# Re-timing six things in a one-core GFNet and mixer kernel: three loads, one store, the filter copies, one fetch, one batch of x, and the stage-1 slots

## The chip, the cores and the metric

One core of one Trainium2 chip. The metric is device time in microseconds (us), from one execution; a kernel was run several times in rounds with the other, and a time quoted alone is the median. Engines: PE (TensorE), DVE (VectorE), ACT (ScalarE), POOL (GpSimd), SP (SyncE, which here only issues transfers). The chip also records the clock that it granted TensorE, as a share of full speed (0.984 on the mean in the kernel before).

## The reference, cut to what matters

```python
def _attn_ref(x, filt_r, filt_i):              # x: 8 x 3136 x 256
    X = np.fft.rfft(x, axis=1)
    Y = X * (filt_r + 1j * filt_i)[None, :, :]
    return np.fft.irfft(Y, n=x.shape[1], axis=1)

def _moe_ref(x, U, V, w_ch1, w_ch2):           # rank 32, hidden 1024
    h = x.transpose(0, 2, 1) @ U @ V
    u = x + h.transpose(0, 2, 1)
    return u + np.maximum(u @ w_ch1, 0.0) @ w_ch2

# reference = _moe_ref(_attn_ref(x, filt_r, filt_i), ...)
```

## The kernel before

The transform of length 3136 = 64 x 49 is split into four matmul stages. Stage 1 (L305) turns x into `asb`, stored to DRAM (`ct1`); stage 2 (L400) reads it back as `a`; VectorE, or GpSimd for some chunks, multiplies with the filter (`uv`, or `ta`, `tb` and their sum `y`); stage 3 (L392) gives `esb`, stored to `ct2`; stage 4 (L592) reads that back as `e`, with the low-rank part `h` in 32 extra rows, and gives `ut`, which feeds the channel matmuls (L603, relu on ScalarE, L636).

The program has one main loop, over blocks of 512 tokens with eight steps each. Each step has one piece of the channel matmuls of batch b; work of later batches is put into steps by a plan. So TensorE's instruction order is fixed, and a late input stops everything behind it: in the kernel before it stood idle for 3.69 us ahead of the matmul at 56.91, until x had come.

```python
    # banks: "w" is ONE bank, used by stage 4 and by stage 1 of batches 2 to 7
    of = {"m": (0, 1), "o": (2, 3), "w": (4,), "e": (7,), ..., "u": (5, 6)}[tag]

    def load_x(b, c, after=None):          # on GpSimd's queue
        ...
            if after is not None:          # a one-element copy: not before `after` is there
                nc.gpsimd.tensor_copy(t[0:1, 0, 0:1], after)
            for h in range(2):
                nc.gpsimd.dma_start(t[h:128:2, ...], dram(x.tensor, ...))

    def st1(b, by=()):                     # stage 1, a generator: one unit per step
        tag = "u" if b == 1 else "w"
        for c in range(3):
            ...                            # 2 matmuls into one bank, copied out to asb
            for h in range(2):
                (nc.gpsimd if (b, c) == (1, 2) else nc.sync).dma_start(dram(ct1[b], ...), asb[...])
            if 2 < b < NB - 1 and c:
                load_x(b + 1, c - 1)       # x of the next batch, from batch 3 on
            yield
        ...

    def make_fc(k, copy):  copy(fc[0:NR, ...], fb[64:NZ, ...])            # L406
    def make_neg(k):       nc.vector.tensor_scalar_mul(fc[64:NZ, ...], fb[64:NZ, ...], -1.0)   # L409
    def make_fa(k, copy):  copy(fa[64:NZ, ...], fb[0:NR, ...])            # L412

    def mid_first():                       # batch 0, before the main loop
        ...
                if k == 7:
                    load_e2(0, 1, 64, 48)
                    load_e2(0, 2)
                    nc.sync.dma_start(sv[0:64, 1024:], s4_d[:, 1024:])
                    load_e2(0, 6)

    def put_h(b, c):                       # the 32 rows of h: e<-h, L559
        nc.vector.tensor_copy(t[64:96], free(h1[b], 64, 96, 0, [[0, n], [1, DM]]))

    # in plan_mid(b, s): when the first three chunks a of batch b are fetched
        for k in range(3):
            at(later(s, (-7, -5, -5)[k] if b == 2 else -8 if b == 3 else -9), fetch, k)

    # the plan
    for n, k in ((9, 3), (10, 5), (11, 2), (12, 4), (13, 0), (13, 1), (15, 6), (15, 7)):
        at(n, make_neg, k)
    for n, k in ((12, 3), (12, 5), (14, 2), (14, 4)):
        at(n, make_fa, k, nc.vector.tensor_copy)
    for n, k in ((6, 0), (7, 1), (8, 6), (9, 7)):
        at(n, make_fc, k, nc.gpsimd.tensor_copy)
    for b in range(1, NB):
        if b == 2:
            plan_st1(b, 18, (0, 3, 4, 5, 7))        # slots: step of the block, 0 to 7
        elif b > 2:
            plan_st1(b, later(start[b - 1], -42 if b == 3 else -60), (0, 3, 4, 5, 7) if b == 3 else (0, 4, 7))
        m = later(start[b - 1], (16, -2, -10, -12)[min(b, 4) - 1])
        ...
    # stage 4 of the next block stands in steps 2 and 6 of a block
```

## Time and profile before

| | before |
|---|---|
| time, 3 runs | 558.71 us (557.92 to 559.39) |
| span of the profiled run | 557.3 us |
| TensorE busy / idle in it | 520.8 / 36.5 us |
| granted clock, mean | 0.984 |

The views: the page gives busy time per engine and, in 40 slices of the span, the tenths of the granted clock. A timeline line has a start, a duration, engine, source line, operation, tiles and shapes, how many instructions are merged, and in brackets the idle time ahead of them with the instruction that ended it. "The gate" stands for the halved clock of the windows view (0.50 from 55.11 to 61.94 in the kernel before). The prediction shows TensorE's lines. Two more turn out to matter. First, VectorE's timeline of the kernel before:

```profile
58.25 0.69 DVE L559 COPY e<-h 32x2048 f16<-32x2048 f16 x1
...
62.70 0.41 DVE L409 TENSOR_SCALAR fc<-fb 49x1024 f16<-49x1024 f16 x1
...
64.16 2.23 DVE L409 TENSOR_SCALAR fc<-fb 49x1024 f16<-49x1024 f16 x1
```

And GpSimd's timeline of the kernel before, over the same time:

```profile
62.61 1.47 POOL L313 DMA_DIRECT2D ct<-asb  x2 [6.06 <-issue]
64.08 2.02 POOL L406 COPY fc<-fb 49x1024 f16<-49x1024 f16 x2
```

One negation takes 0.41 us, the other 2.23 us; the slow one lies beside GpSimd's two copies. And GpSimd does nothing for 6.06 us ahead of the store at 62.61: the store waits for its data, and the two copies behind it wait with it. In just this pause VectorE copies `e<-h` in 0.69 us.

### The profile page before, as it was taken

The numbers are of one execution on the slowest core, as the hardware profiler recorded it, in microseconds if no ns is written. First come the engines' busy times: TensorE is split into PE (matmuls) and PEld (weight loads), VectorE is DVE, ScalarE is ACT, GpSimd is POOL, SyncE is SP. The second block draws the span as 40 slices with busy tenths as digits, with TensorE's granted clock in tenths as the row PEclk, the third lists the DMA queues.
The fourth block names the chain that finished last, engine by engine and source line by source line (L and its number), as shares of the span: only waits on it lengthen the run. The fifth ranks groups of instructions, "written<-read, shape, count | busy, mean of one in ns | idle before, by whom it ended". The sixth has DMA issues, their size and how long they took to land.

```text
span 557.3 us, 11729 instructions
## 1 busy us (share of the span) xinstructions
PE 520.8 (93%) x4540; PEld 374.2 (67%) x4540; DVE 353.7 (63%) x414; ACT 374.9 (67%) x677; POOL 281.3 (50%) x205
## 2 busy tenths in 40 slices
PE   5896879989998889998999999999999999999996
PEld 3643546666675657776776777777786777777775
DVE  7984756637546737669746785758746887643332
ACT  4655437756877567776876788767777567765663
POOL 6856359517995157914684175816563297300000
PEclk9999779999999989999999999999999999999999
DMA  9999496469859749954879468865754554343212
GB/s 195 166 193 211 123 213 181 132 184 194 225 156 193 207 120 221 221 154 126 210 211 234 123 172 219 166 192 159 193 165 124 141 161 126 107 113 114 96 76 85
DMA packets 84391, 91.96 MB, mean 165 GB/s; under 512 B 6725, under 2 KB 68440, under 8 KB 84336
## 3 DMA queue, kind: packets, MB, share of 16 engines
q1 hardware_dynamic: 66560, 74.49, 45.7%
q0 software_dynamic: 17072, 16.26, 19.3%
q8 instruction: 35, 0.57, 0.4%
q10 hardware_dynamic: 704, 0.46, 0.3%
q14 instruction: 20, 0.16, 0.1%
HBM read 57.12 MB, written 49.77 MB: 192 GB/s over the span
## 4 chain that ended last, share of the span: by engine, by line
PE 57%; POOL 2%; DVE 2%; ACT 1%; issue 1%; DMA 1%; ACTq 0%; POOLq 0%
PE psum L636 21%; PE psum L603 21%; PE psum L612 3%; PE psum L400 3%; PE psum L592 3%; PE psum L392 3%; PE psum L305 2%; POOL y L736 1%; PE psum L530 1%; DVE e L559 1%; DMA a<-ct 1%; DVE ut L597 1%; POOL x L187 0%; DVE tb L734 0%; DVE tb L732 0%
## 5 line engine op out<-in xcount | busy, mean ns | idle before, releaser
L607 ACT ACTIVATE hring<-psum 128x512 f16<-128x512 f32 (+1 forms) x416 | 238.1, 576 | 118.7 <-PE psum L603 117.2
L603 PE MATMUL psum<-ut,w1sb 128*128 128x512 f16 (+1 forms) x832 | 242.5, 373 | 2.4 <-DVE ut L597 1.9
L636 PE MATMUL psum<-w2sb,hring 128*128 128x256 f16 x1536 | 231.7, 274 | 0.0
L636 PEld LDWEIGHTS <-hring 128*128 128x128 f16 x1536 | 143.6, 98 | 65.0 <-issue 5.3
L736 POOL TENSOR_TENSOR y<-ta,tb 113x1024 f16<-113x1024 f16 x52 | 111.9, 2158 | 136.5 <-DVE tb L734 91.5
L597 DVE CAST ut<-psum 128x512 f16<-128x512 f32 x94 | 69.6, 741 | 103.3 <-PE psum L592 84.2
L603 PEld LDWEIGHTS <-w1sb 128*128 128x128 f16 x832 | 104.7, 145 | 24.1 <-issue 6.3
L644 DVE COPY och<-psum 128x512 f32<-128x512 f32 x96 | 66.1, 689 | 54.3 <-PE psum L612 53.6
L370 ACT CAST esb<-psum 98x512 f16<-98x512 f32 x128 | 75.0, 587 | 22.8 <-PE psum L392 17.2
L612 PE MATMUL psum<-idn,ut 128*128 128x128 f16 x392 | 54.0, 219 | 0.0
L309 ACT CAST asb<-psum 128x512 f16<-128x512 f32 x76 | 44.8, 589 | 12.3 <-PE psum L305 11.4
L730 DVE TENSOR_TENSOR ta<-psum,fb 113x1024 f16<-113x1024 f32 x37 | 45.1, 1218 | 9.0 <-PE psum L400 7.8
L592 PEld LDWEIGHTS <-e 96*128 96x128 f16 x752 | 34.5, 97 | 23.6 <-issue 6.3
L732 DVE TENSOR_TENSOR tb<-psum,fc 49x1024 f16<-49x1024 f32 x37 | 45.4, 1226 | 1.0
L734 DVE TENSOR_TENSOR tb<-psum,fc 49x1024 f16<-49x1024 f32 x37 | 45.1, 1218 | 1.0
L400 PE MATMUL psum<-a,w2t 98*128 98x512 f16 x120 | 37.1, 386 | 7.6 <-DMA a<-ct 2.9
L592 PE MATMUL psum<-sv,e 96*128 96x64 f16 x752 | 37.3, 192 | 5.0 <-DMA e<-ct 1.9
L612 PEld LDWEIGHTS <-ut 128*128 128x128 f16 x392 | 38.5, 98 | 4.9
L730 POOL TENSOR_TENSOR ta<-pc,fb 113x1024 f16<-113x1024 f16 x15 | 32.4, 2159 | 16.7 <-ACT pc L740 16.6
L305 PE MATMUL psum<-x,wf 128*128 128x256 f16 x168 | 32.7, 280 | 7.4 <-DMA x<-in_x_dram 4.5
L392 PE MATMUL psum<-y,g 113*98 113x512 f16 x98 | 37.4, 381 | 2.2 <-POOL y L736 1.2
L187 POOL DMA_DIRECT2D x<-in_x_dram x48 | 31.1, 661 | 5.1 <-DMA w1sb<-in_moe_w_ch_dram 3.1
(112 smaller groups left out, 385.8 us busy)
## 6 DMA issues: line engine op xcount, KB each, us to landing
out_dram<-och SPq DMA_DIRECT2D x47, 512.0 KB
ct<-esb SPq DMA_DIRECT2D x64, 196.0 KB
x<-in_x_dram POOLq DMA_DIRECT2D x48, 256.0 KB, 7.7
e<-ct SPq DMA_DIRECT2D x46, 256.0 KB
a<-ct SPq DMA_DIRECT2D x56, 196.0 KB
ct<-asb SPq DMA_DIRECT2D x40, 256.0 KB
w1sb<-in_moe_w_ch_dram POOLq DMA_DIRECT2D x1, 512.0 KB, 7.6
w2sb<-in_moe_w_ch_dram POOLq DMA_DIRECT2D x1, 512.0 KB, 9.7
```

Source lines behind the costliest of these rows:

```text
L370: nc.scalar.copy(esb[b, k][:, 2 * half:2 * half + 2, :].rearrange("p s d -> p (s d)"), pe[0:98])
L392: nc.tensor.matmul(pe[0:98], g3[0:NZ, m, :], v, start=(n == 0), stop=(n == len(parts) - 1))
L400: nc.tensor.matmul(pz, w, a, start=True, stop=True)
L592: nc.tensor.matmul(pu[:, 64 * i:64 * i + 64], e2[b, c][:, i, 128 * dh:128 * dh + 128], sv[:, 64 * r:64 * r + 64], start=(i == 0), stop=Tru ...
L597: (nc.scalar.copy if gr is groups[0] and dh else nc.vector.tensor_copy)(o, v)
L603: nc.tensor.matmul(ph[:, 0:n], w1sb[:, dh, :, t], gr.ut[:, dh, 0:n], start=(dh == 0), stop=(dh == 1))
L607: nc.scalar.activation(h[:, 0:n], ph[:, 0:n], RELU)
L612: nc.tensor.matmul(o[:, dh * 128:dh * 128 + 128], gr.ut[:, dh, t0:t0 + n], idn, start=False, stop=(dh == 1), skip_group_check=True)
L636: nc.tensor.matmul(o, gr.h[tt][:, i * 128:(i + 1) * 128], w2sb[:, tt, :], start=(tt == 0), stop=False, skip_group_check=True)
L644: nc.vector.tensor_copy(gr.och[:, 2 * y:2 * y + 2, :].rearrange("p j d -> p (j d)"), gr.pc)
L730: eng.tensor_mul(ta, p[0:NZ], va)
L736: nc.gpsimd.tensor_add(ys[k], ta, tb)
```

## The change

The intent: take away the waits of TensorE that the trace shows, by moving what is issued when. No matrix work is added or removed. (A) three loads of SyncE leave the rush in which x of batch 1 arrives; (B) batch 1's last stage-1 store goes to SyncE, and six negations and two filter copies on VectorE are spread to later steps; (C) batch 2's middle starts a step later; (D) x of batch 4 is held until batch 3's first chunk `a` has come; (E) stage-1 units leave slot 3, where they stood behind a stage 4, for slot 1, and batches 2 to 4 use slots 0, 1, 4, 5, 7.

```diff
@@ st1 @@
-                (nc.gpsimd if (b, c) == (1, 2) else nc.sync).dma_start(
+                nc.sync.dma_start(                                          # B
-            if 2 < b < NB - 1 and c:
+            if 3 < b < NB - 1 and c:                                        # D
                 load_x(b + 1, c - 1)
@@ mid_first @@
-                    load_e2(0, 2)                                           # A
-                    nc.sync.dma_start(sv[0:64, 1024:], s4_d[:, 1024:])
-                    load_e2(0, 6)
@@ plan_mid @@
-            at(later(s, (-7, -5, -5)[k] if b == 2 else ...), fetch, k)
+            at(later(s, (-7, -6, -6)[k] if b == 2 else ...), fetch, k)      # C
+        if b == 3:                                                          # D
+            x4 = later(s, -4)
+            at(x4, lambda: load_x(4, 0, a2[0][0:1, 0:1]))
+            for c in range(1, 4):
+                at(x4 + 1, load_x, 4, c)
@@ the plan @@
+    at(5, load_e2, 0, 2)                                                    # A
+    at(5, lambda: nc.sync.dma_start(sv[0:64, 1024:], s4_d[:, 1024:]))
+    at(5, load_e2, 0, 6)
-    for n, k in ((9, 3), (10, 5), (11, 2), (12, 4), (13, 0), (13, 1), (15, 6), (15, 7)):
+    for n, k in ((9, 3), (10, 5), (17, 2), (19, 4), (32, 0), (33, 1), (35, 6), (36, 7)):   # B
         at(n, make_neg, k)
-    for n, k in ((12, 3), (12, 5), (14, 2), (14, 4)):
+    for n, k in ((12, 3), (12, 5), (19, 2), (20, 4)):                       # B
         at(n, make_fa, k, nc.vector.tensor_copy)
-            plan_st1(b, 18, (0, 3, 4, 5, 7))
+            plan_st1(b, 18, (0, 1, 4, 5, 7))                                # E
-            plan_st1(b, later(start[b - 1], -42 if b == 3 else -60), (0, 3, 4, 5, 7) if b == 3 else (0, 4, 7))
-        m = later(start[b - 1], (16, -2, -10, -12)[min(b, 4) - 1])
+            plan_st1(b, later(start[b - 1], -42 if b == 3 else -46 if b == 4 else -60), (0, 1, 4, 5, 7) if b < 5 else (0, 4, 7))
+        m = later(start[b - 1], (16, -1, -10, -12)[min(b, 4) - 1])          # C
... (also in st1: the last two loads of x, with the same 3 < b)
```

More of the change, by code (lines that the diff above doesn't have):

```diff
@@ L323, in st1 @@
             last()
-            if 2 < b < NB - 1:
+            if 3 < b < NB - 1:
                 load_x(b + 1, 2)
@@ L793, in plan_mid @@
         for k in range(3):
-            at(later(s, (-7, -5, -5)[k] if b == 2 else -8 if b == 3 else -9), fetch, k)
+            at(later(s, (-7, -6, -6)[k] if b == 2 else -8 if b == 3 else -9), fetch, k)
+        if b == 3:
[3 more added lines that the diff above has]
+                at(x4 + 1, load_x, 4, c)
         for k in range(8):
```

## The prediction

> **What bounds the kernel now.** I read the page first, then the waits of TensorE alone, its timeline around each, and last the windows view over the stretches where the clock was halved. The page says that TensorE is the bound:
>
> ```profile
> PE 520.8 (93%) x4540; PEld 374.2 (67%) x4540; DVE 353.7 (63%) x414; ACT 374.9 (67%) x677; POOL 281.3 (50%) x205
> PEclk9999779999999989999999999999999999999999
> ```
>
> No other engine is over 67%, and from slice 20 on TensorE is at 9 nearly everywhere. The change alters no matrix work (4540 matmuls before and after), so it can gain only what TensorE loses: 557.3 - 520.8 = 36.5 us of idle time, and the clock's dips, the digits 7, 7 and 8. TensorE's timeline shows the waits that this change can touch (start, duration, instruction, and in brackets the idle time before it and what ended it):
>
> ```profile
> 56.91 0.59 PE L305 MATMUL psum<-x,wf 128*128 128x256 f16 x2 [3.69 <-DMA x<-in_x_dram]
> ...
> 70.16 0.59 PE L400 MATMUL psum<-a,w2t 98*128 98x512 f16 x2 [1.44 <-DMA a<-ct]
> ...
> 73.94 1.01 PE L400 MATMUL psum<-a,w2t 98*128 98x512 f16 x2 [2.32 <-DVE uv L759]
> ...
> 87.37 0.39 PE L592 MATMUL psum<-sv,e 96*128 96x64 f16 x8 [0.51 <-ACT asb L309]
> ...
> 123.78 0.39 PE L592 MATMUL psum<-sv,e 96*128 96x64 f16 x8 [1.93 <-DMA e<-ct]
> 127.61 0.38 PE L603 MATMUL psum<-ut,w1sb 128*128 128x512 f16 x1 [1.12 <-DVE ut L597]
> ...
> 178.52 0.38 PE L392 MATMUL psum<-y,g 113*98 113x512 f16 x1 [0.91 <-POOL y L736]
> 184.79 0.59 PE L400 MATMUL psum<-a,w2t 98*128 98x512 f16 x2 [1.50 <-DMA a<-ct]
> 198.14 0.38 PE L305 MATMUL psum<-x,wf 128*128 128x256 f16 x2 [1.56 <-DVE ut L597]
> ```
>
> Smaller ones beside these: 0.80 us for x at 50.12 and 0.82 us for ut at 168.96. L305 is stage 1, L400 stage 2, L392 stage 3, L592 stage 4; L603 is the first channel matmul. The windows view then shows what a wait costs a second time (stretch, length, TensorE busy, ..., clock, DMA share, GB/s):
>
> ```profile
> 51.70:55.11 3.41, 1.30 (x14) 0.82 (x12) 2.06 (x4) 1.50 (x4) 1.18 (x2) 1.00 1.14 224
> 55.11:61.94 6.83, 5.04 (x18) 2.81 (x19) 2.86 (x5) 1.78 (x3) 1.44 (x2) 0.50 0.52 159
> 68.76:72.18 3.42, 1.46 (x8) 0.87 (x8) 3.29 (x7) 0.64 (x2) 1.59 (x4) 1.00 0.65 213
> 72.18:79.00 6.82, 5.07 (x16) 2.42 (x16) 2.89 (x4) 0.99 (x2) 2.98 (x5) 0.50 1.05 200
> 119.96:123.38 3.42, 1.89 (x15) 1.18 (x12) 1.75 (x4) 1.79 (x3) 0.00 (x0) 1.00 0.48 126
> 195.06:198.47 3.41, 1.57 (x19) 1.15 (x18) 3.32 (x5) 1.35 (x3) 0.98 (x1) 1.00 0.77 203
> 198.47:201.88 3.41, 3.41 (x15) 1.84 (x14) 0.18 (x1) 2.12 (x4) 1.15 (x1) 0.50 0.55 185
> ```
>
> After a 3.41 us window in which TensorE was busy for 1.30, 1.46 or 1.57 us, the clock is 0.50 for one or two windows; after one with 1.89 us it is not. Half of the busy time in the slow stretches is lost: 2.5 + 2.5 + 1.7 = 6.7 us.
>
> [...] Here the DMA share is 1.14 in 51.70:55.11 with both in flight, so a load on SyncE's queue delays x on GpSimd's. [...] one filter negation took 2.23 us at 64.16 beside a GpSimd copy of 2.02 us at 64.08, another alone 0.41 us.
>
> **The change, part by part.**
>
> *A. Three loads later.* e (256 KB), the rest of sv (64 x 2112 x 2 bytes = 270 KB) and e2l (32 KB) are issued by SyncE at 46 to 47.8 us, while GpSimd's x of batch 1 comes in; the x that ends the 3.69 us wait was issued at 46.93 and landed at 56.77. At 48 to 52 SyncE's queue moved 574 KB, so just these loads, in about 2.2 us of all 16 engines. They now follow the two last stores of block 1 (about 53 us in the old time). x then lands some 2 to 2.5 us sooner and the 0.80 us wait falls to about 0.2: gain 2.9 us. Some 2 us of waiting stays, so I give the gate's 2.5 us a 40% chance to go: 1.0. Stage 4 of block 2 needs the moved loads about 3.6 us after x arrives; they land about then: cost 0.5. Net 3.4 us.
>
> *B. Store on SyncE, negations spread.* GpSimd issued block 2's stores at 62.61 and they landed at 65.97 and 67.31; only then could SyncE fetch a (67.32), hence the 1.44 us. [...] The 2.32 us wait is VectorE: from 67.13 to 72.62 it works off eight negations and copies of 0.38 us each, two ut and one och copies, and the multiplication that frees stage 2's banks starts at 72.66. Without six of the eight it starts when the matmul ends; about 0.5 us of wait is inherent (the multiplication is 1.23 us, the next stage 2 about 0.9 us behind): gain 1.8. With 3.2 us of idle time gone the gate's 2.5 us goes too. Net 5.7 us.
>
> *C. Batch 2's middle a step later.* The order of SyncE's queue shows the first fetch of batch 2 (116.63) now behind batch 1's last esb store (117.05) and its e loads; esb was ready at 116.09, so the store and the e load move 0.9 us ahead of a 1.93 us wait. The first multiplication no longer stands before the ut copy that TensorE waits 1.12 us for. Net 2.0 us.
>
> *D. x of batch 4 held.* Seven x loads at 165.86 to 175.4 fill the DMA engines (share 1.07 over 168 to 182). Batch 3's last store, issued at 172.56, lets SyncE fetch a only at 180.41, hence the 1.50 us. Held until a has come, the loads cannot delay it: 1.5. GpSimd's y is no longer behind 3.1 us of their issue: 0.9. Stage 1 of batch 4 begins 16 steps later, away from step 103 where it followed a stage 4 (1.56, and the gate's 1.7), and batch 3 leaves slot 3 at 168.96: 0.8. Gain 6.5 us. The loads now meet batch 2's last stores and the first e load: cost 1.0.
>
> *E. Stage 1 in slots 0, 1, 4, 5, 7.* Stage 4 stands in slots 2 and 6 and shares one PSUM bank with stage 1. Leaving slot 3 takes away waits for ut, but a unit in slot 1 or 5 stands one step ahead of a stage 4, which waits for ScalarE to empty the bank: the 0.51 us at 87.37, as copies of 0.58 us queue up. The three such cases in the old trace lost 0.41 to 0.67 us against the usual spacing. From the two plans I count them: batch 2 from 3 to 5, batch 3 from 2 to 5, batch 4 from 0 to 5. Ten more at 0.5 us: cost 5.0.
>
> Sum: 3.4 + 5.7 + 2.0 + 6.5 - 1.0 - 5.0 = 11.6 us of gain, which would give 547.1. Some new wait usually appears that I can't name, so I take off 1.4: **548.5 us** (-1.8%).
>
> **Rivals.** (1) *The new slots eat more.* ScalarE is at 11 of 14 us in these stretches; if relus and esb copies pile up, each adjacency may cost 0.8 us and E 8 us: 551.5. For it: all three old cases waited. Against: a plain copy is 0.58 us. (2) *The held loads collide.* x of batch 4 now runs beside batch 2's end, where stage 4 needs e by about 192; if e is 3 us late and the gate trips again: 553. For it: the DMA share there is already 0.72. Against: the same transfers ran before, only in another order. (3) *A is hidden anyway*: if x is limited by its own queue, the 3.69 us wait stays and the moved loads come late for block 2: 3 to 4 us less, 552. For it: that queue alone fills the engines at 46 to 48. (4) *All works and the gate never trips*: 544.
>
> **Range and chances.** A single rival makes 551 to 553, two together 555; the good case is 544. The range is 543.5 to 555. Faster by over 2% means under 547.5, just under my sum before the reserve, so I give it 0.40; within 2% 0.59; slower 0.01, as no part adds work.
>
> **What the new profile should show.** A: the x wait near 55 at 1 to 2.5 us, no new e or sv wait over 1 us at stage 4 of block 2. B: no a wait near 65, stage 2's second half waiting under 1 us, clock 1.00 there. C: the e wait near 115 at about 1 us. D: no a wait before batch 3's stage 2, no dip of the clock near 190. E: about ten more waits of 0.4 to 0.7 us of L592 for asb. The prediction is wrong if TensorE's idle time falls by over 15 us, if the adjacency waits sum to over 8 us, or if a new DMA wait of over 3 us appears.

## The result, and the profile after

The changed kernel took **564.50 us** (564.07 to 567.27, 4 runs) where the kernel before took 558.32 us (556.69 to 559.39, 4 runs of both rounds together). The ratio is 1.0124, 95% interval 1.0082 to 1.0165. Ratios here are the mean time of one kernel's fast runs over the mean of the other's of the same rounds, so not quite the ratio of the medians. So it is within 2%, but slower, and outside the predicted range of 543.5 to 555.

In the changed kernel and in e1 to e5, e10 and e15, L600 is the first channel matmul (L603 before), L589 stage 4 (L592), L556 `e<-h` (L559), L756 the multiplication `uv` (L759), L733 and L731 the sum `y` and the product `tb` (L736, L734); the other runs have the numbers of before, and up to L412 all agree. The page of the changed kernel, busy times and clock:

```profile
PE 521.1 (93%) x4540; PEld 373.7 (66%) x4540; DVE 362.8 (65%) x414; ACT 374.4 (67%) x677; POOL 280.4 (50%) x204
PEclk9997899999999989999999999999999999999999
```

TensorE is as busy as before (520.8), so the span of 562.3 us holds 41.2 us of idle time instead of 36.5. VectorE is 9.1 us busier with the same 414 instructions: some of them have become longer. TensorE's timeline of the changed kernel, at the places that correspond to the prediction's lines and at the new waits:

```profile
62.74 0.59 PE L305 MATMUL psum<-x,wf 128*128 128x256 f16 x2 [4.18 <-DVE asb L309]
...
72.09 0.59 PE L400 MATMUL psum<-a,w2t 98*128 98x512 f16 x2 [0.60 <-DMA a<-ct]
...
74.00 0.59 PE L400 MATMUL psum<-a,w2t 98*128 98x512 f16 x2 [0.44 <-DVE uv L756]
...
84.53 0.59 PE L400 MATMUL psum<-a,w2t 98*128 98x512 f16 x2 [3.77 <-DVE uv L756]
...
108.98 0.59 PE L400 MATMUL psum<-a,w2t 98*128 98x512 f16 x2 [1.34 <-DVE uv L756]
...
127.22 0.39 PE L589 MATMUL psum<-sv,e 96*128 96x64 f16 x8 [1.10 <-DMA e<-ct]
147.22 0.59 PE L400 MATMUL psum<-a,w2t 98*128 98x512 f16 x2 [0.58 <-DVE tb L731]
175.03 0.38 PE L400 MATMUL psum<-a,w2t 98*128 98x512 f16 x1 [1.28 <-DVE tb L731]
197.76 0.39 PE L589 MATMUL psum<-sv,e 96*128 96x64 f16 x8 [2.57 <-DMA e<-ct]
```

The nine waits that the prediction's lines show sum to 14.98 us. At the same places 3.23 us are left: none for x (the matmul at 56.08 starts at once), 0.60 for a, 0.44 for uv, 0.51 for asb, 1.10 for e, 0.58 for y, none of the other three. So 11.75 us of known waits were removed. And 13.72 us of waits that were not there before came in six places: 4.18, 3.77, 1.34, 0.58, 1.28 and 2.57. These two numbers leave 2.0 of the 4.7 us by which the idle time grew; most of the rest is stage 4's wait for `asb`, 4.4 us in 13 places where it was 1.3 us in 3. The question that follows is where the six come from.

VectorE's timeline of the changed kernel just ahead of the first three:

```profile
57.29 4.67 DVE L556 COPY e<-h 32x2048 f16<-32x2048 f16 x1
...
80.99 2.23 DVE L412 COPY fb<-fb 49x1024 f16<-49x1024 f16 x1
...
104.98 2.69 DVE L409 TENSOR_SCALAR fc<-fb 49x1024 f16<-49x1024 f16 x2
```

GpSimd's timeline of the changed kernel at those times:

```profile
57.43 3.98 POOL L406 COPY fc<-fb 49x1024 f16<-49x1024 f16 x4
...
80.75 2.18 POOL L729 TENSOR_TENSOR tb<-pc,fc 49x1024 f16<-49x1024 f16 x1
...
105.09 2.29 POOL L733 TENSOR_TENSOR y<-ta,tb 113x1024 f16<-113x1024 f16 x1 [4.32 <-PE psum L609]
```

The same `e<-h` copy that took 0.69 us now takes 4.67, beside four GpSimd copies that run without the pause of before: with the store gone to SyncE, nothing holds them back. The bank that TensorE waits for is emptied only behind it: VectorE's copy to `asb` starts at 61.99, and the matmul that waited 4.18 us at 62.74. Later, the spread copies stand beside GpSimd's filter multiplications.

The windows view of the changed kernel (stretch, length, busy time of PE, PEld, DVE, ACT, POOL with counts, clock, DMA share, GB/s) shows the second price:

```profile
58.71:62.13 3.42, 0.00 (x0) 0.00 (x0) 3.39 (x2) 0.15 (x1) 2.70 (x3) 1.00 0.92 237
62.13:65.54 3.41, 2.80 (x12) 1.62 (x12) 2.48 (x5) 0.60 (x1) 0.00 (x0) 0.50 0.14 28
```

After a window with no TensorE work at all the clock is at half, and a pair of L600 takes 1.06 us (at 63.12) instead of 0.59 (at 57.53); likewise from 198.66 to 202.08, after one with 0.90 us of work, the one with the 2.57 us wait. It was so also from 45.06 to 51.89, ahead of any step of the main loop, where both programs are nearly alike; there the traces differ among themselves by up to 4 us. To see what belongs to the change I read off when ScalarE ends the relu of each step in both traces, and take the lag of after against before:

| relu of step | lag, us | what lies in between |
|---|---|---|
| 4 | +3.9 | start, and the halved clock at 45 to 52 |
| 8 | -1.8 | before has the x wait and then its halved clock, after has neither |
| 12 | +2.8 | the 4.18 us wait, halved clock |
| 20 | -2.1 | the a and uv waits are gone |
| 24 | +1.6 | the 3.77 us wait |
| 44 | +4.3 | the 1.34 us wait, slots of batch 2 |
| 52 | +1.6 | part C |
| 96 | +1.8 | tb waits, then no a wait |
| 104 | +3.0 | e wait and halved clock |
| 128 | +5.1 | slots of batch 4 |

From step 132 on the lag stays at 5.08. The table also warns: 3.1 of the 5.1 us are there at step 0, so one pair of traces does not size a part; below, sizes come from timed rounds and mechanisms from traces.

### The profile page after: what moved, and what is told of

Same layout as the page of the kernel before. It is cut to its first block, busy times and chain, and to the rows that moved or that the text cites.

```text
span 562.3 us, 11720 instructions
## 1 busy us (share of the span) xinstructions
PE 521.1 (93%) x4540; PEld 373.7 (66%) x4540; DVE 362.8 (65%) x414; ACT 374.4 (67%) x677; POOL 280.4 (50%) x204
## 4 chain that ended last, share of the span: by engine, by line
PE 71%; DVE 10%; DMA 8%; ACT 5%; POOL 4%; issue 2%; SPq 0%; ACTq 0%; POOLq 0%; DVEq 0%
PE psum L633 24%; PE psum L600 23%; PE psum L400 5%; PE psum L392 5%; PE psum L589 4%; PE psum L609 3%; PE psum L305 2%; DMA ct<-esb 2%; DMA x<-in_x_dram 2%; DMA e<-ct 2%; DVE ut L594 2%; DVE tb L729 2%; ACT asb L309 2%; DVE e L556 2%; ACT hring L604 1%
## 5 line engine op out<-in xcount | busy, mean ns | idle before, releaser
L600 PE MATMUL psum<-ut,w1sb 128*128 128x512 f16 (+1 forms) x832 | 242.0, 373 | 1.3 <-DVE ut L594 0.7
L733 POOL TENSOR_TENSOR y<-ta,tb 113x1024 f16<-113x1024 f16 x52 | 112.2, 2164 | 140.8 <-DVE tb L731 111.7
L600 PEld LDWEIGHTS <-w1sb 128*128 128x128 f16 x832 | 104.6, 145 | 23.0 <-issue 6.7
L589 PEld LDWEIGHTS <-e 96*128 96x128 f16 x752 | 34.6, 98 | 30.2 <-issue 11.3
L589 PE MATMUL psum<-sv,e 96*128 96x64 f16 x752 | 37.6, 193 | 9.6 <-ACT asb L309 4.4
L731 DVE TENSOR_TENSOR tb<-psum,fc 49x1024 f16<-49x1024 f32 x37 | 45.1, 1218 | 1.0
L305 PE MATMUL psum<-x,wf 128*128 128x256 f16 x168 | 32.4, 277 | 4.7 <-DVE asb L309 4.6
```

The source lines that it names most:

```text
L589: nc.tensor.matmul(pu[:, 64 * i:64 * i + 64], e2[b, c][:, i, 128 * dh:128 * dh + 128], sv[:, 64 * r:64 * r + 64], start=(i == 0), stop=Tru ...
L600: nc.tensor.matmul(ph[:, 0:n], w1sb[:, dh, :, t], gr.ut[:, dh, 0:n], start=(dh == 0), stop=(dh == 1))
L733: nc.gpsimd.tensor_add(ys[k], ta, tb)
```

## The experiments

All gave correct results. "us" for a ratio means the ratio less 1, times the kernel before's median in the same rounds. Jobs ran on different chips, each with its own runs of before.

### The 4.18 us wait and part B: e1, e2, e3, e4

My theory was that some of VectorE's copies and negations take longer when GpSimd works beside them ("the overlap" below), as the kernel before has it: a negation of 2.23 us beside two GpSimd copies, one of 0.41 alone. The rival was that VectorE merely has too much to do, or that another wait would take the place anyway. In the expectations of e1 to e4, e9 and e11 the first range is the theory's, the second the rival's.

**e1: GpSimd's four copies earlier.** The changed kernel, with

```diff
-    for n, k in ((6, 0), (7, 1), (8, 6), (9, 7)):
+    for n, k in ((0, 0), (1, 1), (2, 6), (3, 7)):
         at(n, make_fc, k, nc.gpsimd.tensor_copy)
```

> The changed kernel (564.5 us), with one thing moved: GpSimd's four filter copies fc 0, 1, 6 and 7 stand at steps 0 to 3, ahead of the store of al on GpSimd's queue, where in the changed kernel they ran at 57.43 to 61.41, beside VectorE's copy e<-h, which took 4.67 us in place of 0.69. [...] e<-h is back at 0.7 us, TensorE's wait of 4.18 us for asb near 62.7 is under 0.6, and the halved clock after it (62.13 to 65.54) goes: 559 to 561 us. Rival, the order on SyncE's queue (the three later loads make block 2 late): the wait stays where it is or turns into one for e or sv of the same size, 563 to 565.

Measured: 563.13 us, ratio 1.0114 (1.0078 to 1.0149). The `e<-h` copy takes 1.19 us, and TensorE's timeline of e1 reads:

```profile
58.15 0.38 PE L305 MATMUL psum<-x,wf 128*128 128x256 f16 x2 [0.69 <-DVE asb L309]
...
62.19 0.58 PE L589 MATMUL psum<-sv,e 96*128 96x64 f16 x8 [2.25 <-DMA sv<-s]
```

So the copies do cause the 4.18 us (0.69 is left), without a single instruction taken from VectorE. But stage 4, reached sooner, now waits 2.25 us for `sv`, one of the three moved loads, and the clock is halved again (a pair of L600 takes 1.06 us at 63.42, 0.60 at 67.31): a wait handed on, and hardly any time won. So the wait follows the theory, and the time (563 to 565 us) the rival, which had foreseen a wait for e or sv instead.

**e2: negations and copies back at their old steps**, in the changed kernel.

```diff
-    for n, k in ((9, 3), (10, 5), (17, 2), (19, 4), (32, 0), (33, 1), (35, 6), (36, 7)):
+    for n, k in ((9, 3), (10, 5), (11, 2), (12, 4), (13, 0), (13, 1), (15, 6), (15, 7)):
-    for n, k in ((12, 3), (12, 5), (19, 2), (20, 4)):
+    for n, k in ((12, 3), (12, 5), (14, 2), (14, 4)):
```

> The changed kernel with the negations and the two fa copies back at the old steps 11 to 15. [...] in the changed kernel fa at 80.99 took 2.23 us beside a GpSimd multiplication and two negations at 104.98 took 2.69, so that TensorE waited 3.77 and 1.34 us for uv; these two waits are under 0.6 here, an uv wait of 1 to 2.3 us near 74 comes back: 561 to 563 us. Rival, stage 1's slots (ScalarE's queue is what delays uv and asb): the 3.77 us wait stays, 564 or more.

Measured: 560.15 us, 1.0059 (1.0024 to 1.0093), so 3.6 us less than the changed kernel (1.0124 - 1.0059). TensorE's timeline of e2:

```profile
59.50 0.59 PE L305 MATMUL psum<-x,wf 128*128 128x256 f16 x2 [3.29 <-DVE asb L309]
72.09 0.59 PE L400 MATMUL psum<-a,w2t 98*128 98x512 f16 x2 [2.25 <-DVE uv L756]
```

The old uv wait is back, the 3.77 and 1.34 us waits are gone. Spreading traded one wait of 2.25 us for two that take 5.1 us together.

**e3: the store back on GpSimd. e4: store and negations back**, both in the changed kernel.

```diff
-                nc.sync.dma_start(
+                (nc.gpsimd if (b, c) == (1, 2) else nc.sync).dma_start(
```

> The changed kernel with batch 1's last stage-1 store back on GpSimd's queue. [...] GpSimd again stops for this store between its copies, so only two of them meet e<-h; it takes 2 to 2.7 us, the wait near 62.7 is 1.5 to 2.5 us, and the wait for a of some 1.4 us before stage 2 is back: 562 to 564.5 us. Rival, SyncE's order: with the store off SyncE's queue the fetches of a come earlier, and the time is under 561.

> The changed kernel with both undone, the store and the negations: what is left are the three later loads, batch 2's step, the held x of batch 4 and the slots. [...] 558.5 to 561 us[...]. If the slots and the held loads are what costs, still 563 or more.

Measured: e3 564.09 us, 1.0134 (1.0095 to 1.0173); e4 558.35 us, 1.0022 (0.9987 to 1.0057). With the store on GpSimd `e<-h` is at 1.64 us in e3 and 2.45 us in e4, the wait behind it at 1.15 and 1.95 us: the pause does shield it in part. In time the store alone is worth nothing (e3 against the changed kernel) to 2 us (e4 against e2). All of part B costs about 5.7 us (1.0124 - 1.0022 of 556.4), where I had predicted a gain of 5.7.

### The parts alone: e5, e6, e7, e8

Each is the kernel before with one part of the change, as in the diff above: e5 part A, e6 part C, e7 part D with batch 4 in slots 0, 3, 4, 5, 7 (before: 0, 4, 7), e8 part E for batches 2 and 3.

> The kernel before with the three loads later alone. Prediction's part A: the x wait of 3.69 us shrinks to 1 to 2.5 us, 3.4 us faster (ratio 0.994). Theory after the runs so far (the wait is only handed on): the x wait shrinks, but VectorE's e<-h copy now meets GpSimd's filter copies and stage 4 of block 2 waits 1.2 to 2.3 us for sv, as in the runs with the store back: within 1.5 us of the kernel before (ratio 0.998 to 1.003).

> The kernel before with batch 2's middle a step later alone. Part C: the e wait near 124 falls from 1.93 to about 1 us and the ut wait of 1.12 goes, 2.0 us faster (0.9965). Rival: the later multiplications of batch 2 stand before a stage 2 near 147 and 175, where the changed kernel shows new waits of 0.6 and 1.3 us for tb: gain under 0.5 us (0.999 to 1.002).

> The kernel before with batch 4's x held and its stage 1 later alone (old slots 0, 3, 4, 5, 7 for batches 2, 3 and 4). Part D: the waits for a (1.50), y (0.91) and ut (1.56) and one halved window (1.7) go, minus 1 us of collision and 3 units in slot 5 at 0.5: 4 us faster (0.993). Rival (2) of the prediction, which the changed kernel's wait of 2.57 us for e at 197.76 and its halved clock there speak for: the e wait of 2.5 to 3.2 us and one or two halved windows (1.7 to 3.4 us) come in their place: within 1.5 us of before (0.998 to 1.003).

> The kernel before with slots 0, 1, 4, 5, 7 for batches 2 and 3 alone (batch 4 as before). Part E by the count: batch 2 from 3 to 5 and batch 3 from 2 to 5 units ahead of a stage 4, at 0.5 us each 2.5 us, minus 0.8 for the wait at 168.96: 1.7 us slower (1.003). If ScalarE piles up (0.8 us each): 3.2 us slower (1.006). If the author's intent holds: 1 us faster (0.998).

| | time, us | ratio (95%) | us | predicted |
|---|---|---|---|---|
| before in these rounds | 557.20 | | | |
| e5, A | 553.85 | 0.9932 (0.9900 to 0.9964) | -3.8 | -3.4 |
| e6, C | 554.38 | 0.9951 (0.9922 to 0.9981) | -2.7 | -2.0 |
| e7, D | 557.90 | 1.0026 (0.9998 to 1.0054) | +1.5 | -3.2 |
| e8, E without batch 4 | 559.61 | 1.0049 (1.0017 to 1.0081) | +2.7 | +1.7 |

(Predicted for e8: the five extra units of batches 2 and 3 at 0.5 us, less the 0.8 us credited under D for batch 3's slot. For e7: D's 6.5 without this 0.8, less 1.0 for the collision and 1.5 for three units that e7 has in slot 5; its expectation of 4 us kept the 0.8.) One run of e5 is left out as slow: its profiled run took 2988.2 us at a recorded clock of 1.0. Its trace says where: TensorE is busy for 2976.2 us and starts the next instruction 2.56 us after a pair of channel matmuls (478.54 to 481.10), where e15, the same kernel, needs 0.43 (479.24 to 479.67), while a relu on ScalarE takes 572 ns as always (576 before). So TensorE alone was slow, by about six times, and the recorded clock doesn't show it. For the waits this trace is of no use; e15 looked again.

e6 did what was foreseen: the e wait is 0.63 us and the 1.12 us wait for ut is gone. e7 is the clear miss. SyncE's timeline of the kernel before (start, time of issue; `ct<-esb` are batch 2's last stage-3 stores):

```profile
182.89 1.09 SPq L377 DMA_DIRECT2D ct<-esb  x2
187.51 0.48 SPq L552 DMA_DIRECT2D e<-ct  x1
```

SyncE's timeline of e7:

```profile
179.18 1.33 SPq L377 DMA_DIRECT2D ct<-esb  x2
187.62 0.48 SPq L552 DMA_DIRECT2D e<-ct  x1
```

and what it cost, in TensorE's timeline of e7:

```profile
194.66 0.41 PE L592 MATMUL psum<-sv,e 96*128 96x64 f16 x8 [3.30 <-DMA e<-ct]
```

The fetch of a, ahead of these, is at 175.44 instead of 180.41, as intended, and by step 96 e7 leads by about 2.2 us. The last stores go out 3.7 us earlier too, but e can still be loaded only at 187.6. From the end of their issue to this load 7.1 us pass (180.51 to 187.62), where it was 3.5 (183.98 to 187.51); the held x, issued from 179.12 on, is in flight beside them, and the windows view has the DMA share at 0.97 to 1.23 from 180.5 to 187.5. Stage 4 comes sooner and waits for it, and the clock halves (0.55 on the mean from 194.60 to 198.10). In the end the lead is gone.

In e8 the waits of stage 4 for `asb` are 2.5 us in 8 places (1.3 in 3 before), so they explain 1.2 of the 2.7 us. TensorE's timeline of e8 shows another:

```profile
124.44 0.59 PE L592 MATMUL psum<-sv,e 96*128 96x64 f16 x8 [3.52 <-DMA e<-ct]
```

It was 1.93 us. Batch 2's last stage-1 store now goes out at 114.31 instead of 111.67, ahead of the fetch and of batch 1's last esb store, which are both 0.6 us later.

### Is it the overlap, or VectorE's load? e9

The changed kernel, with six negations and two copies on ScalarE at the same late steps.

```diff
-        nc.vector.tensor_scalar_mul(fc[64:NZ, ...], fb[64:NZ, ...], -1.0)
+        if k in (3, 5): nc.vector.tensor_scalar_mul(...)
+        else:           nc.scalar.mul(fc[64:NZ, ...], fb[64:NZ, ...], -1.0)
-        at(n, make_fa, k, nc.vector.tensor_copy)
+        at(n, make_fa, k, nc.vector.tensor_copy if k % 2 else nc.scalar.copy)
```

> The changed kernel with six of the eight spread negations and the fa copies of filters 2 and 4 on ScalarE, at the same steps; nothing else differs. [...] GpSimd's multiplications no longer meet a VectorE copy there, the uv waits of 3.77 and 1.34 us fall under 0.6 and the time falls from ratio 1.0124 to between 1.003 and 1.008. Rival, ScalarE is what holds stages 1 and 2 (slots theory): its queue gets 8 us longer, asb waits grow, and the ratio stays at 1.010 or more.

Measured: 561.60 us, 1.0106 (1.0079 to 1.0132). The 3.77 and 1.34 us waits are gone (at most 0.61 left for uv), while GpSimd's work is the same. So VectorE's copies made those two waits. e9 takes away their load and their meeting with GpSimd at once, so it can't part the theory from the rival here; the changed kernel's trace can. Alone such a copy takes about 0.38 us (0.76 for two at 67.92 in the kernel before). The negation at 80.20 and the copy at 80.99 take 0.76 and 2.23, so by this estimate 2.2 of the 3.77 us are the overlap and up to 0.8 the load; the two negations at 104.98 take 2.69 instead of 0.76, which is more than the 1.34 us wait. And the time, 1.0106, is the one that the rival named: ScalarE pays for it, as the view of TensorE's waits in e9 shows (us in total, times, longest):

```profile
PE psum L592 <- ACT asb L309: 6.2, 13, 1.7
```

It was 4.4 in 13 with 0.7 in the changed kernel. And `e<-h` took 3.88 us again, since GpSimd's copies were left where they were.

### Putting the good parts together: e10, e11

e10 is the kernel before with A and C. e11 is that, with the store on SyncE, GpSimd's copies early as in e1, four of the negations on ScalarE at steps 12, 14, 26 and 30, and everything else of B, D and E as before.

```diff
+    (e11 on top of A and C)
+    make_fc by GpSimd at steps 0, 1, 2, 3
+    make_neg at (9, 3), (10, 5), (11, 2), (12, 4) on VectorE; (12, 0), (14, 1), (26, 6), (30, 7) on ScalarE
+    batch 1's last stage-1 store by nc.sync
```

> The kernel before with the three loads later and batch 2's step, the two parts that gained alone (0.9932 and 0.9951). If they are independent: 0.986 to 0.990. If the gate decides (a wait taken from one place only moves a halved window): 0.992 or more.

> The run before it plus the store on SyncE with GpSimd's filter copies moved ahead of al, and negations 0, 1, 6 and 7 on ScalarE, 2 and 4 at the old steps on VectorE. [...] the a wait of 1.8 us goes, the uv wait of 2.3 falls to about 0.8, one halved window fewer: ratio 0.978 to 0.984. Rival, the wait is handed on to sv (2.25 us in the run with the copies early): 0.985 to 0.990.

Measured: e10 551.39 us, 0.9931 (0.9898 to 0.9965), no more than A alone on another chip: A and C do not simply add (product 0.988). e11 **548.19 us** (547.46 to 549.72), 0.9863 (0.9839 to 0.9887); it beats both kernels. The page of e11, busy times and clock:

```profile
PE 513.6 (94%) x4540; PEld 371.5 (68%) x4540; DVE 352.3 (65%) x410; ACT 378.4 (69%) x681; POOL 279.8 (51%) x203
PEclk9999999999999999999999999999999999999999
```

No slice falls below 9. TensorE is busy 7.2 us less than before for the same matmuls, all through the clock (0.999 on the mean, 0.984 before), and idle 32.1 instead of 36.5 us; `e<-h` takes 0.80 us. The wait for `sv` came as in e1 (2.07 us at 60.71), and the ratio is the one that the rival named, not the theory's 0.978 to 0.984. So the same store, moved with GpSimd's copies kept away from `e<-h`, belongs to a faster kernel; in the changed kernel it let four of them run beside it (4.67 us).

### Part D again: e12, and batch 4's slots: e13

e12 is e7, but x of batch 4 held until batch 2's first e has come, instead of batch 3's first a.

```diff
-            at(x4, lambda: load_x(4, 0, a2[0][0:1, 0:1]))
+    at(97, lambda: load_x(4, 0, e2[2, 0][0:1, 0, 0:1]))     # the other three at 97 too
```

> The kernel before with batch 4's x held until batch 2's first e has arrived (seven steps later than in the change) and its stage 1 later, old slots. If what cost part D is the collision of the held loads with batch 2's last stores and e loads: the e wait of 3.30 us near 194.7 and the halved window are gone, the gain of 2.2 us before it stays, ratio 0.993 to 0.998. If it is batch 4's denser slots: 1.001 or more, and no large e wait.

Measured: 555.80 us, 1.0006 (0.9978 to 1.0035). The 3.3 us wait for e is gone (from the last stores to the load of e 2.6 us pass, 178.50 to 181.12), so the time of the held loads decides it, but such a wait comes one batch later, 3.24 us ahead of the stage 4 at 250.96, again with the clock at half (0.50 from 249.94 to 256.80). There the load of e comes 4.6 us after the store before it (242.66 to 247.29; before 2.1), yet the DMA share is only 0.06 to 0.07 from 245.30 to 246.80, the share of one busy engine of sixteen. So this is not the crowding of e7; what held that engine up was not settled. e13 is e7 with batch 4's units in slots 0, 1, 4, 5, 7 instead of 0, 3, 4, 5, 7.

```diff
-    ... (0, 3, 4, 5, 7) if b < 5 else (0, 4, 7))
+    ... (0, 3, 4, 5, 7) if b == 3 else (0, 1, 4, 5, 7) if b == 4 else (0, 4, 7))
```

> The kernel before with x of batch 4 held and batch 4's stage-1 units in slots 0, 1, 4, 5, 7 (batches 2 and 3 as before). If the new slots of batch 4 cost what the changed kernel's trace suggests, this is 2 us slower than the hold with the old slots (ratio 1.0026 there), so about 1.006, with three to five waits of L592 for asb in batch 4 of 0.4 to 0.6 us each; if the slots are free and the lag there came from something else, the ratio stays at 1.0026.

Measured: 560.49 us, 1.0079 (1.0040 to 1.0119), 0.5% above e7; the intervals touch. Between the traces, steps 108 to 128 took 1.4 us more in e13, and the asb waits rose from 2.0 us in 5 to 2.8 in 8. So slot 1 in place of slot 3 seems to cost in batch 4 too, some 1.4 (traces) to 2.9 us (rounds); slot 5 stands in both.

### Do C and E add? e14

The kernel before with C, and E for batches 2 and 3.

> The kernel before with batch 2's middle a step later and the slots 0, 1, 4, 5, 7 for batches 2 and 3. Alone these were -2.7 us and +2.7 us. If the slots cost by the shared bank, the sum holds: ratio 1.000, asb waits of about 2.5 us against 1.3 before. If they cost by SyncE's queue (al's store ahead of the fetch of a, so the last esb store and e come late), the later middle takes that away: e waits at most 1.5 us near 124, ratio about 0.997.

Measured: 560.30 us (556.69 to 563.38), 1.0104 (1.0061 to 1.0148); both expectations were missed. The e wait is 1.01 us, so C does repair SyncE's order. But TensorE's timeline of e14 has two waits:

```profile
143.29 0.59 PE L400 MATMUL psum<-a,w2t 98*128 98x512 f16 x2 [0.58 <-DVE tb L734]
...
171.09 0.38 PE L400 MATMUL psum<-a,w2t 98*128 98x512 f16 x1 [1.28 <-DVE tb L734]
```

They are the two tb waits of the changed kernel, to the hundredth. All waits of stage 2 for tb sum to 2.5 us here, to 1.3 us with C alone, to 0.6 us with E alone and 0.5 before. The first can be followed: with C, VectorE's second product stands behind the ut copy of a stage 4 (in e6 ut at 138.55, the product at 139.32), where before it came 1.9 us after the first. With E a stage-1 unit stands ahead of that stage 4, which waits 0.51 us for the bank (138.82 in e14), so ut and both products are later, and one unit less lies between them and the next stage 2. With C alone this wait for tb is 0.39 us, with E alone there is none. The 1.2 us of tb are a part of what C and E cost together. Another new wait lies beside C: 1.27 us for x at 136.07 in e14, 1.49 at 136.18 in e6, none there in the kernel before or with E alone; as it is 0.47 in e10, its cause is not shown. The rest of the 1.04%, in runs of which the traced one was the fastest, is open.

### Part A again: e15, and one more wait: e16

e15 is e5, one look.

> The loads moved, nothing else; one look for its trace. If the gain of 3.8 us is the wait for x and the gate, the x wait is at most 1.5 us (3.69 before) and the clock is not halved right after it, time about 552 to 554 us. If it is the wait alone, the halved clock at about 55 to 62 is still there.

Measured: 557.07 us in one run, above the expected 552 to 554 and no faster than before in these rounds (555.51); one run of unknown state doesn't overturn e5's five, but it doesn't confirm their gain either. No wait for x is left, but A alone already makes the first of the six new waits. VectorE's timeline of e15:

```profile
55.34 2.73 DVE L556 COPY e<-h 32x2048 f16<-32x2048 f16 x1
```

with GpSimd's copies at 55.49 to 57.52, and TensorE's timeline:

```profile
58.84 0.38 PE L305 MATMUL psum<-x,wf 128*128 128x256 f16 x2 [2.23 <-DVE asb L309]
```

With x earlier, `e<-h` falls into GpSimd's copies; before, it fell into their pause. The clock is halved behind this wait as well (a pair of L600 takes 1.06 us at 60.24, 0.59 at 59.06). So part of A's own gain went to the overlap.

e16 is e11 with no stage-1 unit of batch 4 on step 103:

```diff
-            while s % 8 not in slots or small(s):
+            while s % 8 not in slots or small(s) or s == 103:
```

> The best version so far (e11) with batch 4's stage-1 unit kept off step 103, where it waits 1.56 us for the copy ut of a stage 4 just before. If that wait is freed, 1.3 to 1.6 us less: 546.7 us where e11 had 548.2, ratio 0.984; if the next waits take it over, the ratio stays at 0.986.

Measured: 549.19 us, 0.9885 (0.9855 to 0.9914). The 1.56 us wait of L305 for ut is gone, and the first channel matmul behind it waits 1.35 us for the same ut. From the relu of step 0 to the end the traced run took 497.5 us, e11's 498.8; the rest is the start, 4 us longer in this trace. But about 1.1 of these 1.3 us lie ahead of step 60, where the two plans are the same; from step 90 on e16 gains 0.2 us. The expected 1.3 to 1.6 us are not there.

## Why the prediction was wrong, point by point

**What bounds it**: held. TensorE's busy time did not move (521.1), and everything happened in its idle time and its clock.

**A**: right on the size in e5's rounds (-3.8 against -3.4; e15's single run shows no gain) and on the x wait, wrong on what would be left: none of the expected 2 us for x, but 2.23 us for `e<-h` (e15). "No new e or sv wait" held in the changed kernel only because the wait behind `e<-h` came first (4.18 us); e1 shows `sv` 2.25 us late.

**B**: this is the step that failed most, 11.4 us out (-5.7 predicted, +5.7 measured). The prediction's sentence was "Without six of the eight it starts when the matmul ends", and that came true: 0.44 us are left of 2.32. It said where the eight copies go away from, and never asked what they would stand beside. The row stood in its own text: a negation of 2.23 us beside GpSimd, 0.41 alone (the 2.02 us given there for "a GpSimd copy" are two copies, x2). It was put down as a fact of the old place, and not applied to the new ones (GpSimd's multiplications at 80.75 and 105.09), nor to the GpSimd copies that the departing store set free. e1, e2 and e9 each show a part of it. It also misread the stretch from 67.13 to 72.62: the timeline has ten negations and copies there, of which eight moved, and one ut copy, not eight and two; the gain of 1.8 us held all the same. The 1.44 us for the wait for a rested on an estimate that no trace shows; 0.60 is left of it. That the gate's 2.5 us would go was also wrong; the clock was at half in other windows (62.13 to 65.54, 198.66 to 202.08).

**C**: right (-2.7 against -2.0), alone, though its trace has new waits too (in e6 1.49 us for x at 136.18 and 1.26 for ut at 192.15), which went unforeseen, and loses the 1.50 us wait for a, which was put down to D. Beside E it made two waits for tb (e14).

**D**: about 5 us out (+1.5 against -3.2). The gain up to step 96 was there, 2.2 us. The term mis-sized was the collision, "cost 1.0": it was a wait of 3.30 us in e7 and 2.57 us in the changed kernel, with a halved clock behind it. Rival 2 described exactly this and stayed outside the sum. The 1.56 us put down for step 103 are doubtful as well: in e16 the same move handed 1.35 of such a wait to the next matmul.

**E**: ten more units were counted, and stage 4 of the changed kernel waits for asb in 13 places, 4.4 us in all, the longest 0.7. That is 3.1 us above before's 1.3 us in 3, or 0.31 us for each of the ten, where 0.5 was put down. So the adjacency was put too high. In timed rounds E nevertheless cost more than its terms: 2.7 us (e8) where they give 1.7, and 1.4 to 2.9 us (e13) where they give 1.0 for two units, so 4.1 to 5.6 against 2.7; the other three units of batch 4 are in e7. The rest came for other reasons: SyncE's order, and, beside C, tb.

The parts measured, -3.8, -2.7, +1.5, +2.7, +2.9 and, for B, +5.7, sum to +6.3 us, and the ratio 1.0124 is +6.9. That closeness is partly luck, as A with C and C with E do not add. The prediction's own alarms did not ring: the first watched for idle time that falls by over 15 us, and it rose by 4.7; the adjacency waits are 4.4 and not 8 us, no new DMA wait in the changed kernel exceeds 3 us. They watched for the named rivals, and the largest part of the loss came on an engine pair that none of them named.

**Still open**: the rest of e14's loss, what makes the store ahead of e12's wait at 250.96 late, whether A alone gains (e5 against e15), e5's slow run, whether the store alone costs 0 or 2 us, and after which waits the clock is halved.

## What to carry to other kernels

When an instruction is moved, look up not only what it leaves but what it will run beside (`e<-h` took 0.69 us in GpSimd's pause and 4.67 beside its copies): for VectorE and GpSimd, list the other engine's instructions at the new place, and ask which pause shielded it at the old one. A wait that is removed lets the next consumer arrive earlier, so for each wait ask when the next input lands (`sv` in e1, `e` in e7, ut in e16). Time parts alone and in pairs: the known waits did go, 11.75 of 14.98 us, and the new ones were larger.

## What the traces show of the overlap and the clock

- The overlap: `e<-h` took 0.69 us in GpSimd's pause and 4.67 beside four of its copies, a negation 0.41 alone and 2.23 beside two. By its recorded start `e<-h` began at 57.29 in the changed kernel, ahead of the first of the four (57.43 to 61.41, 3.98 us), and ended at 61.96, after the last; in e15 the same with two (2.73 us). What makes it longer, and whether it had begun its work at the recorded start, no run shows.
- Merely re-timing VectorE's own work, with nothing moved between engines, cost 3.77 and 1.34 us of new waits; ScalarE as the way out was paid there (the longest wait for `asb` 1.7 us in e9, 0.7 without).
- The clock: windows with 0.90, 1.30, 1.46 and 1.57 of 3.4 us busy were followed by half the clock, and also one with 1.82 of 3.41 us (41.65 to 45.06 in the changed kernel), while one with 1.89 of 3.42 us was not. Nor were two with 1.56 and 1.50 us (79.20 to 82.61 and 82.61 to 86.02 in the changed kernel), though the 3.77 us wait lies in them; in e1 the same wait lies in the 3.41 us up to 82.63, of which 0.61 us were busy, and a pair of L600 at 82.69 took 1.06 us instead of 0.60. So busy time between 1.5 and 1.9 us does not decide it. Having no dip was worth 7.2 us of busy time in e11.
- e5's run of 2988.2 us, beside 550.8 to 554.4 us in five others: 2.56 us from a pair of channel matmuls to the next instruction instead of 0.43, TensorE busy for 2976.2 us, at a recorded clock of 1.0. It was not explained.
